# Last inverse-DFT stage of a long convolution for row pairs n2 and 98 - n2, with host-side layouts of the large operands

## The chip, the cores and the metric

The kernel runs on one core of one Trainium2 chip. The core has a matrix engine (PE, with its weight loads shown as PEld), three engines for elementwise work (DVE, ACT and POOL), and SP, which here only issues the transfers between the chip's main memory and the on-chip buffer. All transfers of this kernel stand in SP's one queue, in the order of the program; sixteen DMA engines carry them out. The metric is the device time of the core in microseconds; less is better.

## The reference

Two parts follow each other. The first is a gated long convolution over 12480 positions for 4 batches and 128 channels, done by FFT; the second is a feed-forward layer on the 49920 resulting rows.

```python
h_filt = (np.maximum(pos_emb @ w1, 0.0) @ w2) * np.exp(-0.01 * pos)[:, None]
u = x * v
Uf = np.fft.rfft(u, n=2 * S, axis=1)
Hf = np.fft.rfft(h_filt, n=2 * S, axis=0)
y = np.fft.irfft(Uf * Hf[None, :, :], n=2 * S, axis=1)[:, :S, :]
x2 = (x * y).reshape(B * S, D)
h = x2 @ w_in                                   # 128 -> 2048
g = h * np.clip(h + 3.0, 0.0, 6.0) / 6.0
return g @ w_out                                # 2048 -> 128
```

## The kernel before

**The transform.** The sequence is cut into two halves k of 98 and 97 rows (`R`) of 64 positions (`N1`), so that a position has a row index n2 and a column index n1. A transform has four matrix stages. `first_stage` (L223) multiplies 98 rows n2 of one channel by cosine and sine tables: the output is 64 rows for the cosine part and 64 for the sine part, each a float32 matmul on one half of the array's columns. `second_stage` (L242) goes over n1 with a table per frequency k2, 99 frequencies in 25 chunks of four. `products` multiplies with the filter's spectrum: two copies on ACT that swap real and imaginary parts (L474, L475), four products on DVE (L495 to L498), additions on POOL (L502). `third_stage` (L517) goes back over n1 and ACT copies the result into the buffer `z` (L525). `back` (L532) turns four columns of `z` with the identity so that k2 lies on the partitions, and `split_r` (L136 on ACT, L137 on DVE) splits the turned values into a high and a low part for matmuls of the reduced float32r type. `fourth_stage` (L551) takes eight columns: three products (high x high, high x low table, low x high) for the cosine and the sine part, six one-pass matmuls into one PSUM bank for 98 rows n2. ACT copies the bank to `y` (L557), and after 16 columns `store` (L567, L569) writes three blocks of 32 rows to `yd` and the one or two leftover rows to `ye`.

**The order.** Everything is emitted in a hand-written order and each engine keeps it. `filter` computes the filter's spectrum from `pos_emb` (64 turns L293, 16 hidden matmuls L305, then L327, which spreads over channels) and writes it to `hd`. Then come eight periods g, each for 2 batches x 32 channels. In a period, `chunk` goes through the 25 frequency chunks of group g; between the chunks the loop of `period` runs 32 steps n: a `back` of group g-1, sometimes a `fourth_stage` of group g-1, some decoding of feed-forward weights on DVE (`weight`, in periods 1 to 6), and after every fourth step a `visit`, which is four first stages of group g+1. x and v are loaded by `load_next` (L415) and multiplied by POOL in `gate_next` (L426). Tables `tab` (L446) are loaded 7 chunks ahead, the spectrum `h` (L459) 4 chunks ahead. `last_turn` does the turns and last stages of the last group, and `Moe.run` the feed-forward part: 98 tiles of 512 rows (two of them of leftover rows), each with 8 steps j of six matmuls up (L764 to L766) and six down (L799 to L803); x, y and the result of a tile are loaded and stored by `load` and `copy`.

**PSUM.** The eight banks are shared out by name: `BANKS = {"s2": 2, "sw": 1, "s3": 1, "ts": 3, "s4": 1}`. A name's banks are handed out in turn, and a matmul that starts in a bank waits until the last reader of the bank before is done. First stages and turns share "ts"; the last stage has "s4".

**Layouts.** x and v arrive as (batch, position, channel), so a load for 32 channels takes pieces of 32 values, 128 bytes; the same holds for the tiles of x and of the result in the feed-forward part.

Of the kernel before, what the change touches and what calls it, by code (L numbers as in the profile page):

```python
# [22 lines left out]

B, S, D = 4, 12480, 128
FO = 64
# [6 lines left out]
L = R[0] * N1  # L32

G = 32
GB = 2
GY = 16
NG = (D // G) * (B // GB)
# [5 lines left out]

NR = 3
REST = [(b, k, r) for b in range(B) for k in range(2) for r in range(32 * NR, R[k])]
# [15 lines left out]
def constants():  # L61
    n2, k2, n1, k1 = np.arange(R[0]), np.arange(K2), np.arange(N1), np.arange(N1)
    th = 2 * np.pi * np.outer(n2, k2) / N2
    c_tab = np.concatenate([np.cos(th), -np.sin(th)], axis=1)
    wt = np.where((k2 == 0) | (k2 == N2 // 2), 1.0, 2.0) / NF
    d_tab = np.stack([wt[:, None] * np.cos(th.T), -wt[:, None] * np.sin(th.T)], axis=1)
# [5 lines left out]
        [np.concatenate([fr, fi], axis=2), np.concatenate([-fi, fr], axis=2)], axis=0  # L72
    )
    ph = ph - (2 * np.pi / NF) * np.outer(k2, k1)[None]
    gr, gi = np.cos(ph), np.sin(ph)
    g_tab = np.concatenate(
# [16 lines left out]

@with_exitstack
def hyena_moe(ctx, tc, x, v, pos_emb, w1, w2, w_in, w_out, c_tab, d_tab, f_tab, g_tab, win_d, ident_d, out):
# [5 lines left out]
    yd = [[dram.tile([NR, 4, 32, 2, N1, GY], F32, name=f"yd{b}_{k}") for k in range(2)] for b in range(B)]  # L101
    ye = dram.tile([len(REST), N1, D], F32, name="ye")
# [8 lines left out]
    def rows(t, b, k, r0, r1):  # L111

        a = t[b, k * L + r0 * N1 : k * L + r1 * N1, :]
        return a.rearrange("(r n) d -> r n d", n=N1)

    left, right = ExitStack(), ExitStack()
    with tc.manual_schedule():
        conv = Conv(tc, nc, left, right, x, v, c_tab, d_tab, g_tab, ident, hd, yd, ye, rows, weights)
# [5 lines left out]
        moe = Moe(ctx, tc, nc, x, wd, yd, ye, out)  # L124
        conv.last_turn(moe)
        right.close()
        moe.run()
# [64 lines left out]
class Conv:  # L192
    def __init__(self, tc, nc, left, right, x, v, c_tab, d_tab, g_tab, ident, hd, yd, ye, rows, weights):
        self.tc, self.nc, self.left, self.right = tc, nc, left, right
        self.x, self.v, self.g_tab, self.ident, self.hd, self.yd, self.rows = x, v, g_tab, ident, hd, yd, rows
# [6 lines left out]
        self.dhi = self.keep.tile([K2, 2, R[0]], F32R, name="dhi")  # L202
        self.dlo = self.keep.tile([K2, 2, R[0]], F32R, name="dlo")
# [4 lines left out]
    BANKS = {"s2": 2, "sw": 1, "s3": 1, "ts": 3, "s4": 1}  # L208
# [38 lines left out]
    def filter(self, pos_emb, w1, w2, f_tab, win_d, ident_d):  # L247
# [11 lines left out]
        dtab = sp.tile([K2, 2, R[0]], F32, name="dtab")  # L259
# [8 lines left out]
        pt = flat[: R[0], : 2 * N1 * FO].rearrange("p (k n i) -> p k n i", k=2, n=N1)  # L268
        pos = [pos_emb[k * L : k * L + R[k] * N1, :].rearrange("(r n) i -> r n i", n=N1) for k in range(2)]

        def load_pos(n0, n1):
            for k in range(2):
                nc.sync.dma_start(pt[:96, k, n0:n1, :], pos[k][:96, n0:n1, :])

        nc.vector.memset(pt[96 : R[0], 1, :NB], 0.0)
        nc.gpsimd.memset(pt[96 : R[0], 1, NB:], 0.0)
        load_pos(0, NB)
        nc.sync.dma_start(self.ident, ident_d)
        for k in range(2):
            nc.sync.dma_start(pt[96 : R[k], k], pos[k][96:])  # L280
        for k in range(2):
            nc.sync.dma_start(w1bd[k * FO : (k + 1) * FO, k * FO : (k + 1) * FO], w1)
        for n in ((NB, 8), (8, 16), (16, 32), (32, N1)):
            load_pos(*n)
# [5 lines left out]
        def turned(n):  # L290
            tp = self.bank("ptT")
            for i in range(NB):
                nc.tensor.transpose(  # L293
                    tp[:, i * R[0] : (i + 1) * R[0]],
                    pt[:, i // 2, n + i % 2 * 2 : n + i % 2 * 2 + 2, :].rearrange("p n i -> p (n i)"),
# [17 lines left out]
        while pend:  # L313
            hidden(*pend.pop(0))
# [552 lines left out]
```

## Time and profile before

| | us |
|---|---|
| median of 3 runs | 3317.9 (3316.59 to 3318.12) |
| the profiled execution | 3315.44 |
| its span, first to last instruction | 3313.7 |
| first L764 (feed-forward part begins) | 1184.75 |
| first and last third-stage copies L525 | 180.0 and 1138.0 |

The page gives, per engine, the time in which it was busy and the number of instructions; forty slices of the span with tenths of busy time; and groups of instructions by source line with their count, total, mean in ns, and the idle time of the engine just before them. A time line row gives the start, the time until the last of the merged instructions ended, the engine, the line, what was written from what, the count, and in brackets the idle time before and what ended it. Matmuls overlap, so their distance from start to start is the price of one, not the duration in the row. A row of the window table gives a window, its length, the busy time and count of PE, PEld, DVE, ACT and POOL, the granted clock of PE as a share, the share of time in which the DMA engines moved data, and GB/s. A row of the waits names who waited for whom, and gives the sum in us, the count and the longest.

### The profile page before, as it was taken

Reading aid. Unit: us, or ns where it says so; the run is one execution under the profiler, and the core shown is the slowest. Engines: PE = TensorE matmul, PEld = TensorE weight load, DVE = VectorE, ACT = ScalarE, POOL = GpSimd, SP = SyncE. Lnnn points to the kernel's source line nnn. Section 1 sums busy time; section 2 is a strip of 40 time slices with the busy share of each in tenths; the row PEclk is TensorE's granted clock in tenths of the full one; section 3 lists DMA queues with packets and bytes.
Section 4 is the critical chain, followed back from the end, with each engine's and each line's share of the span. In section 5 each row is a group of like instructions: output and inputs, shape, how many; then the busy total and the mean of one; then the engine's idle time right before and its main releaser. Section 6 shows DMA issues by size and latency. Waiting matters only on the chain.

```text
span 3313.7 us, 54920 instructions
## 1 busy us (share of the span) xinstructions
PE 3226.8 (97%) x20346; PEld 2764.7 (83%) x20346; DVE 2380.8 (72%) x2837; ACT 2400.2 (72%) x3104; POOL 2108.6 (64%) x1243
## 2 busy tenths in 40 slices
PE   8988999999999999999999999999999999999999
PEld 7988888888888888888888888888888888888887
DVE  5545666666766667777777777777777777777776
ACT  2355666666667677778778787787878777777777
POOL 1166677676776546666666666666666666666666
PEclk9998999999999999999999999999999999999999
DMA  9789989989985522211211222112221112221121
GB/s 208 200 163 187 187 186 193 187 194 186 189 186 168 170 61 39 39 33 34 45 34 34 39 39 39 34 34 38 39 39 37 32 37 39 39 39 32 36 39 23
DMA packets 972127, 296.41 MB, mean 89 GB/s; under 512 B 841962, under 2 KB 938641, under 8 KB 970769
## 3 DMA queue, kind: packets, MB, share of 16 engines
q1 hardware_dynamic: 971860, 292.91, 42.1%
q8 instruction: 160, 2.62, 0.4%
q14 instruction: 107, 0.88, 0.1%
HBM read 224.49 MB, written 68.29 MB: 88 GB/s over the span
## 4 chain that ended last, share of the span: by engine, by line
PE 68%; POOL 0%; DVE 0%; issue 0%; ACT 0%
PE acc L803 11%; PE ph L764 11%; PE acc L800 11%; PE ph L765 11%; PE acc L799 11%; PE ph L766 11%; PE s L551 1%; PE ts L532 1%; PE s L517 1%; PE s L242 1%; PE s L532 0%; POOL pa L502 0%; DVE o L816 0%; ACT oT L806 0%; DVE wlo L137 0%
## 5 line engine op out<-in xcount | busy, mean ns | idle before, releaser
L788 POOL TENSOR_TENSOR glo<-g,ghi 128x1024 fp32r<-128x1024 f32 x588 | 1404.3, 2395 | 766.5 <-ACT ghi L786 766.3
L776 DVE SCALAR_TENSOR_TENSOR g<-r,ph 128x1024 f32<-128x1024 f32 (+1 forms) x784 | 949.5, 1211 | 411.1 <-ACT r L774 411.0
L774 ACT ACTIVATE r<-ph,three 128x1024 f32<-128x1024 f32 (+1 forms) x784 | 870.9, 1111 | 274.1 <-PE ph L766 274.0
L786 ACT CAST ghi<-g 128x1024 fp32r<-128x1024 f32 (+1 forms) x784 | 811.0, 1034 | 0.8 <-DVE g L776 0.7
L764 PE MATMUL ph<-xhi,win_hi 128*128 128x512 f32 (+1 forms) x1568 | 608.4, 388 | 0.0
L765 PE MATMUL ph<-xlo,win_hi 128*128 128x512 f32 (+1 forms) x1568 | 608.3, 388 | 0.0
L766 PE MATMUL ph<-xhi,win_lo 128*128 128x512 f32 (+1 forms) x1568 | 608.3, 388 | 0.0
L800 PE MATMUL acc<-ghi,wout_lo 128*128 128x512 f32 (+1 forms) x1568 | 608.0, 388 | 0.0
L799 PE MATMUL acc<-ghi,wout_hi 128*128 128x512 f32 (+1 forms) x1568 | 607.9, 388 | 0.0
L502 POOL TENSOR_TENSOR pa<-pa,pq 128x256 f32<-128x256 f32 (+1 forms) x400 | 312.5, 788 | 274.7 <-DVE pa L496 234.3
L803 PE MATMUL acc<-glo,wout_hi 128*128 128x512 f32 (+1 forms) x1568 | 481.2, 388 | 0.0
L764 PEld LDWEIGHTS ph<-xhi,win_hi 128*128 128x128 f32 x1568 | 294.3, 188 | 60.9 <-DVE g L776 0.2
L799 PEld LDWEIGHTS acc<-ghi,wout_hi 128*128 128x128 f32 x1568 | 294.4, 188 | 60.7
L765 PEld LDWEIGHTS ph<-xlo,win_hi 128*128 128x128 f32 x1568 | 294.5, 188 | 60.5
L766 PEld LDWEIGHTS ph<-xhi,win_lo 128*128 128x128 f32 x1568 | 294.4, 188 | 60.5
L800 PEld LDWEIGHTS acc<-ghi,wout_lo 128*128 128x128 f32 x1568 | 294.3, 188 | 60.4
L803 PEld LDWEIGHTS acc<-glo,wout_hi 128*128 128x128 f32 x1568 | 293.5, 188 | 60.9 <-POOL glo L788 0.7
L495 DVE TENSOR_TENSOR pq<-s,h 128x256 f32<-128x256 f32 (+1 forms) x200 | 84.2, 421 | 284.2 <-issue 106.3
L788 DVE TENSOR_TENSOR glo<-g,ghi 128x1024 fp32r<-128x1024 f32 x196 | 283.6, 1447 | 0.0
L223 PEld LDWEIGHTS ts<-ctab,u 98*64 98x64 f32 (+1 forms) x5120 | 229.4, 139 | 46.4 <-DVE wlo L137 24.9
L223 PE MATMUL ts<-ctab,u 98*64 98x99 f32 (+1 forms) x5120 | 246.8, 254 | 21.3 <-DVE wlo L137 20.8
L517 PE MATMUL s<-pa,tab 128*128 128x128 f32 x1694 | 240.9, 288 | 26.7 <-POOL pa L502 14.8
(72 smaller groups left out, 4060.0 us busy)
## 6 DMA issues: line engine op xcount, KB each, us to landing
tab<-in_g_tab SPq DMA_DIRECT2D x192, 256.0 KB
h<-hd SPq DMA_DIRECT2D x384, 128.0 KB
xt<-in_x SPq DMA_DIRECT2D x64, 384.0 KB
vt<-in_v SPq DMA_DIRECT2D x64, 384.0 KB
yd<-y SPq DMA_DIRECT2D x192, 128.0 KB
xt<-in_x SPq DMA_DIRECT2D x384, 64.0 KB
yt<-yd SPq DMA_DIRECT2D x96, 256.0 KB
out<-o SPq DMA_DIRECT2D x384, 64.0 KB
```

Source lines behind the costliest of these rows:

```text
L223: nc.tensor.matmul(tv[c * N1 : (c + 1) * N1, i, :K2], u[: R[k], 4 * j + i, :], self.ctab[: R[k], c * K2 : (c + 1) * K2], start=True, stop= ...
L502: nc.gpsimd.tensor_tensor(out=x, in0=x, in1=y, op=add)
L764: nc.tensor.matmul(ph[:, i, :ne], self.win_hi[:, sl], hi[:, :ne], start=True, stop=False)
L765: nc.tensor.matmul(ph[:, i, :ne], self.win_hi[:, sl], lo[:, :ne], start=False, stop=False)
L766: nc.tensor.matmul(ph[:, i, :ne], self.win_lo[:, sl], hi[:, :ne], start=False, stop=True)
L774: nc.scalar.activation(r[:, :, :ne], ph[:, :, :ne], AF.Relu, bias=self.three)
L776: nc.vector.scalar_tensor_tensor(out=g[:, :, :ne], in0=r[:, :, :ne], scalar=6.0, in1=ph[:, :, :ne], op0=ALU.min, op1=ALU.mult)
L786: nc.scalar.copy(ghi[:, :, :ne], g[:, :, :ne])
L788: e.tensor_tensor(out=glo[:, :, :ne], in0=g[:, :, :ne], in1=ghi[:, :, :ne].bitcast(F32), op=ALU.subtract)
L799: nc.tensor.matmul(a, self.wout_hi[:, f, :], ghi[:, i, :ne], start=(f == 0), stop=False)
L800: nc.tensor.matmul(a, self.wout_lo[:, f, :], ghi[:, i, :ne], start=False, stop=False)
L803: nc.tensor.matmul(a, self.wout_hi[:, f, :], glo[:, i, :ne], start=False, stop=(f == NFC - 1))
```

## The change

**The last stage.** For real results, the cosine part of the inverse DFT is the same for the rows n2 and 98 - n2 of the two halves' grid, and the sine part differs in sign. The change keeps tables for rows 0 to 49 only (`RH` = 50, padded to 64), computes the two parts into two banks and gets both rows as their sum and their difference. The parities of the frequency k2 are folded into the other tables. The matmuls are float32, without a split into high and low parts; each writes 64 output rows, and the two groups of 8 columns (h) go to the two halves of the array's columns.

```diff
-    BANKS = {"s2": 2, "sw": 1, "s3": 1, "ts": 3, "s4": 1}
+    BANKS = {"s2": 2, "sw": 1, "s3": 1, "ts": 4}
...
     def back(self, g, col):
...
-        if col % 8 == 0:
-            self.pair = [self.wp.tile([K2, 8, 128], F32R, tag=n, name=f"w{n}", bufs=3) for n in ("hi", "lo")]
-        hi, lo = (w[:, col % 8 : col % 8 + 4, :].rearrange("p c m -> p (c m)") for w in self.pair)
-        split_r(nc, hi, lo, t[:K2, :])
-        if col % 8:
-            self.pend.append((g, col - 4, *self.pair))
+        if col % GY == 0:
+            self.w = self.wp.tile([K2, GY, 128], F32, tag="w", name="w", bufs=3)
+        nc.scalar.copy(self.w[:, col % GY : col % GY + 4, :].rearrange("p c m -> p (c m)"), t[:K2, :])
+        if col % GY == GY - 4:
+            self.pend.append((g, col + 4 - GY, self.w))
...
+        g, col, w = self.pend.pop(0)
+        same, other = (self.bank("ts") for i in range(2))
+        for c, t in enumerate((same, other)):
+            for h in range(2):
+                nc.tensor.matmul(
+                    t[64 * h : 64 * h + 64, :],
+                    self.dtab[:, c, :],
+                    w[:, GH * h : GH * h + GH, c * N1 : (c + 1) * N1],
+                    start=True,
+                    stop=True,
+                )
+        y = self.wp.tile([128, 2, N1, GH], F32, tag="y", name="y")
+        same, other = (t.rearrange("p (c n) -> p n c", c=GH) for t in (same, other))
+        o = self.wp.tile([128, N1, GH], F32, tag="o", name="o", bufs=1)
+        nc.scalar.copy(o, other)
+        for i, op in enumerate((ALU.add, ALU.subtract)):
+            nc.vector.tensor_tensor(out=y[:, i], in0=same, in1=o, op=op)
...
+        for h in range(2):
+            e = ch // GH + h
+            for i, p, q, r, n in PARTS:
+                nc.sync.dma_start(self.yd[b][k][q, d // G, r : r + n, e], y[64 * h + p : 64 * h + p + n, i])
+            for i, p, r in ((0, 49, 49), (1, 1, 97)):
+                if r < R[k]:
+                    nc.sync.dma_start(
+                        self.ye[REST.index((b, k, r)), d // GH + e].unsqueeze(0), y[64 * h + p : 64 * h + p + 1, i]
+                    )
```

with `G` = 32, `GY` = 16, `GH` = 8, and the row blocks

```diff
+ROWS = [*range(32), *range(96, 64, -1), *range(32, 49), *range(64, 49, -1)]
+REST = [(b, k, r) for b in range(B) for k in range(2) for r in (49, 97) if r < R[k]]
+PARTS = [(0, 0, 0, 0, 32), (1, 2, 1, 0, 32), (0, 32, 2, 0, 17), (1, 34, 2, 17, 15)]
```

**Its place.** In a period the last stage now stands after every fourth step, right before the visit; one is left over for the next period's first chunk. In the last turn it comes with every fourth turn, which alternate between "ts" and "s2".

```diff
-                if len(self.pend) > 1:
-                    self.fourth_stage(self.pend.pop(0))
-                if g:
                     self.weight(n)
                 n += 1
-                if n % VISIT == 0 and g + 1 < NG:
-                    self.visit(g + 1, n // VISIT - 1)
+                if n % VISIT == 0:
+                    if n > VISIT:
+                        self.fourth_stage()
+                    if g + 1 < NG:
+                        self.visit(g + 1, n // VISIT - 1)
```

**Layouts.** The host hands over x and v by groups, so that a row of a load is 16 channels x 64 positions in one piece; x once more by tiles of the feed-forward part; `pos_emb` already turned; and it takes the result by tiles. The turns of `pos_emb` on PE and their copies on DVE go.

```diff
-                nc.sync.dma_start(t[r0:r1], self.rows(src, b, k, r0, r1)[:, part, d : d + G])
+                nc.sync.dma_start(t[r0:r1], src[g, piece, half, r0:r1])
...
-            self.nc.gpsimd.tensor_tensor(
-                out=u[: R[k], :, part].rearrange("p g n -> p n g"), in0=xt[: R[k]], in1=vt[: R[k]], op=ALU.mult
-            )
+            u = self.gated[-1][:, half * G // 2 : (half + 1) * G // 2, :]
+            self.nc.gpsimd.tensor_tensor(out=u, in0=xt, in1=vt, op=ALU.mult)
...
-        for n in range(0, N1, NB):
-            pend.append((n, turned(n)))
-            if len(pend) > 2:
-                hidden(*pend.pop(0))
-        while pend:
-            hidden(*pend.pop(0))
+        for n in range(0, N1, NB):
+            hidden(n)
...
-        self.copy(xt, self.x, t)
+        nc.sync.dma_start(xt, self.x[t])
...
+                for m in range(len(i)):
+                    a = self.ye[s + m, 4 * j : 4 * j + 4].rearrange("e (h r) c -> r h e c", r=32)
+                    for h in range(2):
+                        cols = slice(64 * m + 32 * h, 64 * m + 32 * h + 32)
+                        nc.sync.dma_start(
+                            y[32 * j : 32 * j + 32, cols].rearrange("r (e c) -> r e c", c=GH), a[:, h]
+                        )
...
-        self.copy(o, self.out, t)
+        nc.sync.dma_start(self.out[t, :, :ne], o[:, :ne])
```

The work that builds these layouts and puts the result back into its order is done in numpy outside the kernel and is not in the time: `by_groups`, `by_tiles`, `by_pairs` and `from_tiles` are reshapes, transposes and copies.

More of the change, by code (lines that the diff above doesn't have):

```diff
@@ L75, in constants @@
     gr, gi = np.cos(ph), np.sin(ph)
+    gr = np.where(oc, -gr, gr)
     g_tab = np.concatenate(
@@ L109, in hyena_moe @@
     ident = const.tile([P, P], F32, name="ident")
-    def rows(t, b, k, r0, r1):
-        a = t[b, k * L + r0 * N1 : k * L + r1 * N1, :]
-        return a.rearrange("(r n) d -> r n d", n=N1)
     left, right = ExitStack(), ExitStack()
     with tc.manual_schedule():
-        conv = Conv(tc, nc, left, right, x, v, c_tab, d_tab, g_tab, ident, hd, yd, ye, rows, weights)
+        conv = Conv(tc, nc, left, right, x, v, c_tab, d_tab, g_tab, ident, hd, yd, ye, weights)
         conv.filter(pos_emb, w1, w2, f_tab, win_d, ident_d)
@@ L192, with __init__ @@
 class Conv:
-    def __init__(self, tc, nc, left, right, x, v, c_tab, d_tab, g_tab, ident, hd, yd, ye, rows, weights):
+    def __init__(self, tc, nc, left, right, x, v, c_tab, d_tab, g_tab, ident, hd, yd, ye, weights):
         self.tc, self.nc, self.left, self.right = tc, nc, left, right
-        self.x, self.v, self.g_tab, self.ident, self.hd, self.yd, self.rows = x, v, g_tab, ident, hd, yd, rows
+        self.x, self.v, self.g_tab, self.ident, self.hd, self.yd = x, v, g_tab, ident, hd, yd
         self.c_tab, self.d_tab, self.weights, self.ye = c_tab, d_tab, weights, ye
@@ L360, in filter @@
                 self.gate_next()
-        split_r(nc, self.dhi, self.dlo, dtab)
         for piece in range(2 * GB):
@@ L409, in load_next @@
         piece, half = divmod(i, 2)
-        k, b, d = self.place(g, piece)
-        xt, vt = ((xv or self.xv).tile([R[0], N1 // 2, G], F32, tag=f"{c}t", name=f"{c}t") for c in "xv")
-        part = slice(half * N1 // 2, (half + 1) * N1 // 2)
+        xt, vt = ((xv or self.xv).tile([R[0], G // 2, N1], F32, tag=f"{c}t", name=f"{c}t") for c in "xv")
         for t, src in ((xt, self.x), (vt, self.v)):
-            for r0, r1 in ((0, 96), (96, R[k])):
-                nc.sync.dma_start(t[r0:r1], self.rows(src, b, k, r0, r1)[:, part, d : d + G])
-        self.loaded.append((k, part, xt, vt, xv is None))
+            for r0, r1 in ((0, 96), (96, R[0])):
+                nc.sync.dma_start(t[r0:r1], src[g, piece, half, r0:r1])
+        self.loaded.append((half, xt, vt, xv is None))
         self.n_loaded += 1
@@ L544, in fourth_stage @@
         piece, ch = divmod(col, G)
         k, b, d = self.place(g, piece)
-        d, ch = d + ch // GY * GY, ch % GY
-        t = self.bank(("s4", "s3")[col // 8 % 2] if g == NG - 1 else "s4")
-        n = 0
-        for wt, dt in ((hi, self.dhi), (hi, self.dlo), (lo, self.dhi)):
-            for c in range(2):
-                nc.tensor.matmul(
-                    t[: R[0], :], dt[:, c, :], wt[:, :, c * N1 : (c + 1) * N1], start=(n == 0), stop=(n == 5)
-                )
-                n += 1
@@ L855 @@
     arrays, args = {}, []
-    given = {n: np.ascontiguousarray(inputs[n]) for n in _INS} | constants()
+    x = np.asarray(inputs["x"])
+    given = {
+        "x": by_groups(x),
+        "v": by_groups(np.asarray(inputs["v"])),
+        "xt": by_tiles(x),
+        "pos_emb": by_pairs(np.asarray(inputs["pos_emb"])),
+    }
+    given |= {n: np.ascontiguousarray(inputs[n]) for n in ("w1", "w2", "moe_w_in", "moe_w_out")} | constants()
     for name, a in given.items():
```

180 lines of the change are left out of this document (78 added, 102 removed).

## The prediction

> **What bounds the kernel now.** I read the page first (busy shares and the forty slices), then the window table by stage, then the time line of PE inside one period, then the waits.
>
> ```profile
> PE 3226.8 (97%) x20346; PEld 2764.7 (83%) x20346; DVE 2380.8 (72%) x2837; ACT 2400.2 (72%) x3104; POOL 2108.6 (64%) x1243
> ...
> PEclk9998999999999999999999999999999999999999
> DMA  9789989989985522211211222112221112221121
> GB/s 208 200 163 187 187 186 193 187 194 186 189 186 168 170 61 39 39 33 34 45 34 34 39 39 39 34 34 38 39 39 37 32 37 39 39 39 32 36 39 23
> ```
>
> The page says PE everywhere, but two regimes lie under it: in the first thirteen slices (83 us each) the DMA engines are nearly full at only some 190 GB/s, afterwards they are almost idle. The window table cuts the span by stage: period 0, periods 1 to 6, period 7, the last turn, the feed-forward part (MoE).
>
> ```profile
> core 0: us, PE busy (x) PEld busy (x) DVE busy (x) ACT busy (x) POOL busy (x), PEclk, DMA share, GB/s
> ...
> 180.00:284.20 104.20, 89.90 (x1002) 85.04 (x1002) 48.40 (x100) 56.70 (x109) 70.58 (x72) 0.93 0.94 178
> 284.20:1049.20 765.00, 716.39 (x6803) 646.88 (x6804) 512.62 (x968) 508.26 (x948) 540.33 (x497) 0.96 0.88 187
> 1049.20:1138.00 88.80, 84.57 (x573) 77.24 (x572) 63.91 (x125) 64.04 (x117) 63.40 (x70) 0.99 0.59 180
> 1138.00:1184.70 46.70, 46.18 (x230) 39.56 (x231) 23.66 (x35) 29.13 (x50) 0.00 (x0) 0.95 0.45 120
> 1184.70:3313.70 2129.00, 2123.09 (x9409) 1758.74 (x9408) 1642.53 (x1369) 1687.16 (x1764) 1404.28 (x588) 1.00 0.19 37
> ```
>
> MoE is PE at full clock with no gap: 9408 matmuls in 2129 us, which the change neither adds to nor takes from. All that can move lies in the first 1185 us. There a period takes 765/6 = 127.5 us, with clock 0.96. How much of that is work? The starts on PE:
>
> ```profile
> 712.84 2.96 PE L223 MATMUL ts<-ctab,u 98*64 98x99 f32 x64
> 715.73 0.94 PE L532 MATMUL ts<-ident,z 128*99 128x128 f32 x4
> 716.51 1.06 PE L517 MATMUL s<-pa,tab 128*128 128x128 f32 x8
> ...
> 718.89 0.70 PE L551 MATMUL s<-whi,dhi 99*98 99x512 f32 x2
> 719.43 0.62 PE L551 MATMUL s<-whi,dlo 99*98 99x512 f32 x2
> 719.89 0.62 PE L551 MATMUL s<-wlo,dhi 99*98 99x512 f32 x2
> 720.35 1.05 PE L517 MATMUL s<-pa,tab 128*128 128x128 f32 x8
> 721.25 1.06 PE L242 MATMUL s<-z,tab 128*128 128x128 f32 x8
> ```
>
> From start to start: a chunk's four third-stage matmuls take 0.90 us (8 records, so a float32 matmul is two passes), a last stage (six one-pass matmuls, 8 columns) 720.35 - 718.89 = 1.46, four first stages (32 matmuls) 715.73 - 712.84 = 2.89, four turns 0.78. A period holds 25 chunks at 2 x 0.90, 32 turns at about 0.7, 16 last stages and 8 visits: 45 + 22 + 23 + 23 = 113 us. Some 14 us per period are waits and a lowered clock. The waits of PE, periods 1 to 6, then period 0:
>
> ```profile
> PE ts L223 <- DVE wlo L137: 20.8, 21, 1.9
> PE s L517 <- POOL pa L502: 10.4, 11, 1.5
> PE s L242 <- DMA tab<-in_g_tab: 9.9, 6, 3.1
> ...
> PE s L242 <- DMA tab<-in_g_tab: 13.2, 8, 3.1
> ```
>
> **The new last stage on PE.** It does 16 columns with four float32 matmuls of 99 rows by 64 output columns, 512 long: eight passes, each on one half of the array. The first stage is the same form, 98*64. Its 64 passes took 2.89 us, 45.2 ns a pass of 99 columns; whole-array passes (L517) take 0.90/8 = 112 ns for 128. Per column 0.456 against 0.879 ns: the two halves run at once. A pass of 512 columns is then worth 45.2 x 512/99 = 0.234 us, eight 1.87, and 0.10 for the change from whole to half array (estimate): 1.97 us against 2 x 1.46 = 2.92. Gain 0.95 each, 64 in all: 8 per period, 7.6 us. Bounds: 1.75 (whole-array speed halved, no overhead) and 3.84 (no overlap).
>
> At its beginning the first stage shows two passes started together:
>
> ```profile
> 712.84 0.31 PE L223 MATMUL ts<-ctab,u 98*64 98x99 f32 x2
> ```
>
> If the two passes of one matmul stand next to each other in the stream and none may start ahead of another, eight passes would take five slots of 0.467 and not four: 2.43 us. The Trainium skill, "TensorE: Matmul & The Clock Gate", Part 3: Packing small matmuls — row/col tiling, says just this of matmuls, "strict FIFO, no reordering"; by it the sum would be 0.46 x 64 = 30 us worse. The pair of first starts above speaks for four slots, so I take 1.97.
>
> **What the other engines lose and gain.** Means of one:
>
> ```profile
> L496 DVE TENSOR_TENSOR pa<-s,h 128x512 f32<-128x512 f32 x192 | 130.7, 680 | 0.0
> L557 ACT COPY y<-s 98x512 f32<-98x512 f32 x128 | 75.1, 586 | 82.4 <-PE s L551 77.0 <-DMA h<-hd 3.1 <-DMA xt<-in_x 0.8
> L137 DVE TENSOR_TENSOR wlo<-ts,whi 99x512 fp32r<-99x512 f32 x244 | 164.1, 683 | 63.6 <-ACT whi L136 62.9
> L426 POOL TENSOR_TENSOR u<-xt,vt 98x1024 f32<-98x1024 f32 x32 | 77.3, 2416 | 51.2 <-DMA vt<-in_v 50.5 <-POOL u L426 0.7
> ```
>
> Per period DVE loses 32 wlo (21.9 us) and gets 16 add/subtract of 128x512, nearest row 680 ns (10.9). ACT keeps 32 copies (w for whi) and does 8 copies o instead of 16 y: -4.7. POOL's u keeps its elements; only its output order changes, price as before. None of these busy times reaches PE's: POOL, the fullest, has 540/6 = 90 us a period.
>
> **The wait that goes and the wait that comes.** Today the first stages wait for a bank that wlo still reads. The long ones:
>
> ```profile
> 355.65 0.91 PE L223 MATMUL ts<-ctab,u 97*64 97x99 f32 x16 [0.52 <-DVE wlo L137]
> 358.44 2.91 PE L223 MATMUL ts<-ctab,u 97*64 97x99 f32 x32 [1.89 <-DVE wlo L137]
> ```
>
> wlo is gone, so 20.8/6 = 3.5 us a period go. But the new last stage takes two of the four "ts" banks and a visit of four first stages follows it at once. Ten banks are handed out per round, so the visit's third first stage gets the bank "same". That is free only after ACT's o (0.59) and both DVE operations (0.62 from start to start, then 0.68): 1.9 us after the last pass ends, while PE is there after two first stages, 2 x 0.72 = 1.4. Wait: about 0.6 us with idle engines (estimate), seven times a period 4.4, plus some 0.8 at the two visits where the weights' decoding has filled DVE: 6.0 us a period. Behind the waiting matmul stand the next chunk's matmuls on PE. Behind the two DVE operations stand the next products (L495 to L498), for which POOL waits. Bounds: 0 (if it hides) and 12 (DVE 1 us late each time).
>
> **The transfers.** x and v came in pieces of 128 bytes and come in rows of 4 KB; pos_emb, the MoE tiles and the result come in long rows too. Around 26 us, where f_tab's long rows run, the engines move
>
> ```profile
> 26.00:30.00 4.00, 4.00 (x22) 2.65 (x21) 1.70 (x3) 2.26 (x5) 0.00 (x0) 1.00 0.99 422
> ```
>
> 422 GB/s against 187 in the periods. So waits for tab go: 9.9/6 = 1.7 us a period, 13.2 in period 0. Clock: 0.96 of 127.5 is 5.1 us lost per period, 0.93 of 104.2 is 7.3 in period 0. I suppose that it sinks where PE idles long; those sources go, short ones come: I take 3.2 and 3.8 back (bounds 0 and all).
>
> What the change adds is issues on SP. Its queue now (xt and vt of one piece; yd three and ye one store; h; tab):
>
> ```profile
> 598.00 5.26 SPq L415 DMA_DIRECT2D xt<-in_x  x2
> 603.30 2.48 SPq L415 DMA_DIRECT2D vt<-in_v  x2
> 605.88 1.45 SPq L567 DMA_DIRECT2D yd<-y  x3
> 607.38 0.69 SPq L569 DMA_DIRECT2D ye<-y  x1
> 608.17 1.29 SPq L459 DMA_DIRECT2D h<-hd  x2
> 609.56 0.54 SPq L446 DMA_DIRECT2D tab<-in_g_tab  x1
> 610.20 1.23 SPq L459 DMA_DIRECT2D h<-hd  x2
> ```
>
> Start to start: h pair 1.36 and tab 0.64, 50 us a period; x and v 7.9 for four, later 32 x 0.50 = 16; weights 3. Stores: 4 last stages of 12 and 4 of 10 are 88 a period (32 before), at yd's 0.50: 44. Sum 113 of the 117.5 that I expect for the period. SP is covered, barely; its loads are ahead by 4 chunks (h) and 7 (tab), so its waits for DVE cost nothing by themselves.
>
> **Start, end and MoE.**
>
> ```profile
> 28.18 2.17 PE L305 MATMUL h<-z,w1bd 128*128 128x392 f32 x6
> 30.18 14.14 PE L327 MATMUL h<-w2bd,ht 128*98 128x128 f32 x128
> ```
>
> The position filter's 64 turns and their copies go. Left are 16 matmuls at 2.00/3 = 0.67 us = 10.7, after the first landing at some 5 us, and about 3 us (estimate) for slower first matmuls and the 3.2 MB to come: L327 starts near 18.7, 11.5 earlier (bounds 8 and 13). In MoE the loads and stores shrink to three per tile, off the path. The tile of eight leftover rows needs 64 loads from ye; now:
>
> ```profile
> 1515.55 1.90 SPq L718 DMA_DIRECT2D yt<-ye  x4
> ```
>
> At 0.48 that is 31 us, against some 31 us from SP's turn to the gate on DVE; 1 us for it (bounds 0 and 12). The last store is one issue, not four: -1.5.
>
> **Sum.** Start -11.5. Period 0: -13.2 - 3.8 = -17. Periods 1 to 6: -7.6 - 3.5 - 1.7 - 3.2 + 6.0 = -10.0 each, -60. Period 7 (15 last stages there, 8 after): 15.8 - 21.9 = -6.1. Last turn (17, then 9): 17.7 - 24.8 = -7.1. End -1.5, MoE +1. Together -102 on a span of 3313.7; the median of the runs, 3317.9, is 4.2 above it: 3216 us.
>
> **Rivals.**
> - Clean periods: the bank wait hides, the clock stays full, half of POOL's waits go. 127.5 - 7.6 - 3.5 - 1.7 - 5.1 - 0.9 = 108.7, or -113 for six: 3163. For it: DVE gets 11 us lighter. Against: o, add and subtract are a chain.
> - Periods stay: the new bank wait and POOL's lateness eat all: -60 falls away, 3276. For it: 10.4 us of POOL waits already now.
> - Five slots: the first-in-first-out order above, +30: 3246. It is the skill's rule just named; the pair of starts is against it.
> - SP becomes the bound. At ye's spacing (608.17 - 607.38 = 0.79) for every store its period is 69 + 70 = 139 us, +21 x 6 = 126: 3342, slower. It binds from (117.5 - 69)/88 = 0.55 us per store, and the kernel is slower than before from about 0.74. For it: 24 of the 88 move a single row, as ye does. Against: ye's row is cut into 64-byte pieces, the new one isn't.
> - The halves don't overlap at 512 columns: 3.84 us each, +120: 3336, slower; it decides from 1.97 + 102/64 = 3.56 us. Against: L223's rate.
>
> **Chances.** Forecast 0.45, clean 0.22, stay 0.12, five slots 0.07, SP 0.10 (half of it slower), no overlap 0.04. The first four and a short SP bind give faster 0.91; same (within 0.2%, 6.6 us, about what a measurement of this kernel can tell) 0.02; slower 0.07. Range 3155 to 3278: both clean and stay periods lie in it, the two slower cases are left out.
>
> **What would show it.** The time line after: a last stage of about 2 us between starts; L327 starting near 19 us; no wait for tab; L223 waiting on DVE's second operation at the third first stage of a visit, 0.6 us; periods of 117 us; MoE still 2129 us. I am wrong if periods stay near 127 (then the wait named there tells which engine), if the last stage takes 2.4 or 3.8, or if SP has no gap left.

## The result, and the profile after

The changed kernel takes 3259.49 us (median, 3254.63 to 3260.52); the kernel before, run beside it, 3317.24 us. The ratio is 0.9827, with a 95% interval of 0.981 to 0.9844. It became faster by 58 us, where 102 had been forecast; the forecast of 3216 us is 43 us too low, and its range of 3155 to 3278 holds the time.

The window table of the changed kernel, cut as the one of before was: period 0, periods 1 to 6, period 7, the last turn, the feed-forward part.

```profile
core 0: us, PE busy (x) PEld busy (x) DVE busy (x) ACT busy (x) POOL busy (x), PEclk, DMA share, GB/s
169.10:261.00 91.90, 84.04 (x1012) 79.92 (x1013) 48.35 (x100) 56.35 (x108) 69.55 (x72) 1.00 0.87 217
261.00:988.20 727.20, 663.99 (x6603) 581.50 (x6602) 480.00 (x872) 475.99 (x899) 515.93 (x497) 0.97 0.73 195
988.20:1074.20 86.00, 79.64 (x539) 66.68 (x538) 53.20 (x107) 58.27 (x109) 63.21 (x70) 0.99 0.54 155
1074.20:1120.90 46.70, 43.36 (x200) 27.96 (x200) 12.21 (x19) 23.92 (x42) 0.00 (x0) 0.95 0.51 170
1120.90:3257.30 2136.40, 2126.49 (x9409) 1760.61 (x9408) 1642.55 (x1371) 1687.37 (x1764) 1404.32 (x588) 1.00 0.12 37
```

Set beside the windows of before, stage by stage:

| us | forecast | measured | |
|---|---|---|---|
| up to period 0 | -11.5 | -10.9 | 180.0 to 169.1 |
| period 0 | -17 | -12.3 | 104.2 to 91.9 |
| periods 1 to 6 | -60 | -37.8 | 765.0 to 727.2, 121.2 each |
| period 7 | -6.1 | -2.8 | 88.8 to 86.0 |
| last turn | -7.1 | 0 | 46.7 to 46.7 |
| feed-forward part and end | -0.5 | +7.4 | 2129.0 to 2136.4 |
| sum | -102 | -56.4 | span 3313.7 to 3257.3 |

The time line of PE inside a period shows a last stage between a turn and a visit:

```profile
541.51 0.84 PE L557 MATMUL ts<-ident,z 128*99 128x128 f32 x4
542.28 1.94 PE L574 MATMUL ts<-w,dtab 99*64 99x512 f32 x8
544.05 2.92 PE L282 MATMUL ts<-ctab,u 98*64 98x99 f32 x64
546.89 0.94 PE L557 MATMUL ts<-ident,z 128*99 128x128 f32 x4
```

From start to start the new last stage takes 544.05 - 542.28 = 1.77 us, four slots, close to the lower bound of 1.75. PE has won more here than forecast. The waits of PE in periods 1 to 6 show where it went:

```profile
PE s L542 <- POOL pa L527: 22.1, 38, 1.6
PE s L301 <- DMA tab<-in_g_tab: 19.1, 11, 3.1
PE ts L557 <- DVE y L586: 15.3, 5, 3.5
PE s L301 <- DVE pa L521: 2.6, 1, 2.6
PE s L542 <- ACT sw L499: 2.3, 1, 2.3
PE s L542 <- ACT z L550: 1.0, 6, 0.2
```

The 20.8 us for wlo are gone, as forecast. But the waits for the tables, which were to vanish, doubled (9.9 before), those for POOL doubled too (10.4 before), and a new one stands in the third row: a turn that waits for y. There is no row in which a first stage (L282) waits for anything. All rows together are 62.6 us, against 48.6 before: the waits grew by 14.

### The profile page after: what moved, and what is told of

The parts are those of the page before. It is cut to its first block, busy times and chain, and to the rows that moved or that the text cites. A ratio compares the mean times of both kernels' runs of the same rounds, so it can differ in the third digit from the quotient of the medians.

```text
span 3257.3 us, 53858 instructions
## 1 busy us (share of the span) xinstructions
PE 3156.4 (97%) x20026; PEld 2667.5 (82%) x20026; DVE 2315.7 (71%) x2691; ACT 2356.5 (72%) x3039; POOL 2079.7 (64%) x1242
## 4 chain that ended last, share of the span: by engine, by line
PE 66%; DMA 1%; SPq 0%; POOL 0%; ACT 0%; issue 0%; DVE 0%; DVEq 0%; ACTq 0%
PE acc L807 11%; PE acc L803 11%; PE acc L804 11%; PE ph L769 11%; PE ph L770 11%; PE ph L768 11%; DMA yd<-y 1%; PE ts L574 0%; PE ts L557 0%; SPq L592 0%; PE s L557 0%; DMA yt<-yd 0%; PE s L542 0%; PE s L301 0%; DMA ye<-y 0%; DMA tab<-in_g_tab 0%
## 5 line engine op out<-in xcount | busy, mean ns | idle before, releaser
L527 POOL TENSOR_TENSOR pa<-pa,pq 128x256 f32<-128x256 f32 (+1 forms) x400 | 290.3, 732 | 247.4 <-DVE pa L521 220.8
L542 PEld LDWEIGHTS s<-pa,tab 128*128 128x128 f32 x1694 | 212.4, 197 | 64.4 <-POOL pa L527 50.0
L741 DVE TENSOR_TENSOR xy<-xt,yt 128x512 f32<-128x512 f32 x96 | 260.3, 2711 | 0.0
```

The costliest lines, as they stand in the source:

```text
L527: nc.gpsimd.tensor_tensor(out=x, in0=x, in1=y, op=add)
L542: nc.tensor.matmul(t[:, i * 128 : (i + 1) * 128], tab[:, i, :], a[:, i].rearrange("p s g -> p (s g)"), start=(n == 0), stop=(n == len(term ...
```

## Experiments

Each kernel was timed in three rounds beside the kernel before. The ratio is to that; the other columns are windows of its trace, cut as above, in us. The kernel before came out between 3317 and 3323 us in these rounds, so a few us between the medians of two rows say little by themselves; the ratios and the windows say more.

| kernel | median | ratio (95%) | to period 0 | period 0 | periods 1 to 6 | period 7 | last turn | feed-forward |
|---|---|---|---|---|---|---|---|---|
| before | 3317.24 | 1 | 180.0 | 104.2 | 765.0 | 88.8 | 46.7 | 2129.0 |
| changed | 3259.49 | 0.9827 (0.981 to 0.9844) | 169.1 | 91.9 | 727.2 | 86.0 | 46.7 | 2136.4 |
| e1 | 3284.57 | 0.989 (0.9874 to 0.9907) | 168.9 | 92.1 | 760.6 | 88.8 | 46.6 | 2127.0 |
| e2 | 3416.14 | 1.029 (1.0275 to 1.0305) | 169.2 | 102.3 | 873.9 | 85.9 | 46.6 | 2133.9 |
| e3 | 3232.24 | 0.9736 (0.9722 to 0.9751) | 168.7 | 92.0 | 712.6 | 85.2 | 42.5 | 2129.5 |
| e4 | 3257.52 | 0.9813 (0.9796 to 0.9829) | 169.2 | 92.0 | 732.2 | 86.0 | 46.9 | 2132.7 |
| e5 | 3259.21 | 0.9808 (0.9792 to 0.9824) | 169.6 | 92.0 | 731.8 | 86.0 | 48.2 | 2135.2 |
| e6 | 3262.4 | 0.9816 (0.9802 to 0.9831) | 169.9 | 92.0 | 732.5 | 85.3 | 42.6 | 2141.7 |
| e7 | 3184.57 | 0.9583 (0.9567 to 0.9599) | 169.1 | 92.0 | 667.1 | 83.1 | 41.6 | 2129.5 |
| c2 | 3209.41 | 0.9657 (0.9642 to 0.9671) | 168.2 | 92.0 | 690.1 | 86.0 | 42.8 | 2128.6 |
| e8 | 3208.5 | 0.9656 (0.9641 to 0.967) | 169.2 | 92.0 | 688.8 | 86.1 | 42.7 | 2128.6 |
| c3 | 3222.27 | 0.9694 (0.9678 to 0.9711) | 184.8 | 91.5 | 688.9 | 85.3 | 42.7 | 2129.5 |
| c4 | 3222.96 | 0.9701 (0.9686 to 0.9715) | 182.1 | 91.5 | 688.4 | 86.0 | 42.9 | 2129.6 |
| c5 | 3204.15 | 0.9645 (0.9629 to 0.9661) | 170.1 | 92.0 | 683.4 | 85.2 | 42.2 | 2128.6 |

### e1: the layouts alone

The kernel before, with the host-side layouts of the change and the old last stage; the core of the edit is

```diff
-                nc.sync.dma_start(t[r0:r1], self.rows(src, b, k, r0, r1)[:, part, d : d + G])
+                nc.sync.dma_start(t[r0:r1], src[g, piece, half, r0:r1])
...
-        self.copy(o, self.out, t)
+        nc.sync.dma_start(self.out[t, :, :ne], o[:, :ne])
```

> The layouts alone: x, v, pos_emb, the feed-forward tiles and the result as in the changed kernel, the last stage and its stores as before (six float32r matmuls for eight columns, four stores per sixteen columns). If the layouts carry the start, period 0 and the waits for tab, as the changed kernel's stages say (-11 at the start, -12 in period 0), and a part of the periods: periods of about 125 us, last turn 46.7 and feed-forward part 2129 us as before, 3277 us in all. If the new last stage carries the gain of the periods as well as most of the rest: periods of 127, some 3292 us.

The time lies between the two expectations. The start (-11.1), period 0 (-12.1) and the end (-2.0) come whole from the layouts. In periods 1 to 6 they bring 4.4 us and no more, though the waits for the tables vanish there; the waits of PE are now

```profile
PE ts L266 <- DVE wlo L180: 20.2, 20, 1.9
PE s L528 <- POOL pa L513: 18.1, 19, 2.3
PE s L528 <- ACT sw L485: 9.2, 4, 2.3
```

The 9.9 us that stood on the tables have moved to POOL (10.4 before) and to ACT's swap (6.5 before). A wait that is removed here comes back at the next engine in the chain.

### e2: the changed kernel with the old loads of x and v

```diff
-                nc.sync.dma_start(t[r0:r1], src[g, piece, half, r0:r1])
+                nc.sync.dma_start(t[r0:r1], self.rows(src, b, k, r0, r1)[:, part, d : d + G])
...
-            self.nc.gpsimd.tensor_tensor(out=u, in0=xt, in1=vt, op=ALU.mult)
+            u = self.gated[-1]
+            self.nc.gpsimd.tensor_tensor(
+                out=u[: R[k], :, part].rearrange("p g n -> p n g"), in0=xt[: R[k]], in1=vt[: R[k]], op=ALU.mult
+            )
```

> The changed kernel, but x and v loaded in pieces of 128 bytes and multiplied as before. If SP's issue is what long rows relieve: h 34, tab 16, x and v 48, stores 33, weights 3 make 134 us of SP a period, so periods of 134 us or more, about 3350 us, slower than before. If only the DMA engines' bandwidth counts: periods near 124, period 0 back at 104 us, about 3290 us.

873.9 / 6 = 145.7 us a period, and one wait of PE makes most of the difference:

```profile
PE s L306 <- DMA tab<-in_g_tab: 131.4, 40, 6.0
```

SP's rows in the time line, added over periods 1 to 6, are 755 us of 873.9 in 1205 issues (before: 666 of 765 in 873; changed: 516 of 727 in 1197). The DMA engines were no fuller than in the kernel before (a share of 0.79 at 164 GB/s, against 0.88 at 187), which speaks for SP being late and against the bandwidth, though SP's issues alone make only 126 of the 145.7 us. The new last stage brings so many stores that, with the old loads, the kernel takes 97 us more than the kernel before beside it (3319.55). All the layouts together bring 4 us in periods 1 to 6 under the old last stage (e1); the long rows of x and v alone bring 147 us (873.9 - 727.2) under the new one.

### e3: half the stores

The rows are put into two blocks of 48 instead of four blocks of 32, 32, 17 and 15, so that a last stage issues six stores instead of ten or twelve, of the same bytes. The feed-forward part loads a tile's y in four issues instead of one.

```diff
-            for i, p, q, r, n in PARTS:
-                nc.sync.dma_start(self.yd[b][k][q, d // G, r : r + n, e], y[64 * h + p : 64 * h + p + n, i])
-            for i, p, r in ((0, 49, 49), (1, 1, 97)):
-                if r < R[k]:
-                    nc.sync.dma_start(
-                        self.ye[REST.index((b, k, r)), d // GH + e].unsqueeze(0), y[64 * h + p : 64 * h + p + 1, i]
-                    )
+            for i in range(2):
+                p = 64 * h + i * (k + 1)
+                nc.sync.dma_start(self.yd[b][k][d // G, RM * i : RM * i + RM, e], y[p : p + RM, i])
+            m = REST.index((b, k, RM))
+            nc.sync.dma_start(self.ye[m : m + 2 - k, d // GH + e], y[64 * h + RM : 64 * h + RM + 2 - k, 0])
```

> The changed kernel with six stores per last stage in place of ten to twelve (48 rows of the sum and 48 of the difference in one store each, the leftover rows 48 and 49 in one), and four loads of y per feed-forward tile instead of one. If SP's many stores hold the y buffers and with them the last turn and the beginning of the feed-forward part: last turn 39 us instead of 46.8, feed-forward part 2129 to 2131 instead of 2136, periods 0 to 1 us shorter; 3244 us. If the chain o, add, subtract sets the last turn: no stage moves by more than 2 us, 3258 us.

It is 27 us faster than the changed kernel: periods 1 to 6 -14.6, the last turn -4.2, the beginning of the feed-forward part -6.9. In periods 1 to 6 no table and no spectrum is waited for any more:

```profile
PE s L542 <- POOL pa L527: 25.6, 40, 2.3
PE ts L557 <- DVE y L586: 17.6, 10, 2.8
PE s L542 <- ACT sw L499: 6.9, 3, 2.3
```

SP's issues are 444 us in 961 instructions here, against 516 in 1197. Neither fills SP. What else held SP stands in its own waits. In every trace of this case the issues on SP raise eight semaphores (counters that an engine can wait for) in strict turn, and all but a few (20 of 2057 in the changed kernel) wait for their own one first: such an issue goes out only when the transfer eight issues before it has landed. So the first of these two rows of the changed kernel, periods 1 to 6, is stores that wait for a load of v issued eight places earlier; the second is stores that wait for their own y:

```profile
SPq L592 <- DMA vt<-in_v: 24.5, 25, 1.8
...
SPq L592 <- DVE y L586: 1.8, 4, 1.1
```

All rows of that table that name a transfer add up to 114 us; all in which a store waits for DVE, to 13. In e3 the rows that name a transfer add up to 59 us, and SP waits 69 us for POOL to free a buffer of x and v (6 in the changed kernel), so there it is ahead. A store takes one of the eight places for nearly as long whatever its size: one row is issued in 0.24 us and has landed 2.7 us after its issue began (median), 32 rows 2.9 us after. So the number of stores costs twice, in issues and in places: 516 + 114 of 727 us in the changed kernel, 444 + 59 of 713 here. Which of the two made the 14.6 us no run separates.

### e4: eleven buffers for the tables

```diff
-NT = 7
+NT = 11
...
-            self.w = self.wp.tile([K2, GY, 128], F32, tag="w", name="w", bufs=3)
+            self.w = self.wp.tile([K2, GY, 128], F32, tag="w", name="w", bufs=2)
```

> The changed kernel with 11 buffers for tab instead of 7 (tables loaded 8 chunks ahead rather than 4), w with two buffers instead of three to make room. If PE's 19 us of waits for tab in periods 1 to 6 come from too short a lead in the quick chunks at a period's start: they fall below 5 us and some of the lowered clock goes, periods 118 us, 3240 us. If the DMA engines are simply full at those moments: the waits stay or turn into waits of DVE for h, 3255 us or more.

`NT` counts buffers. A table is held from the second stage to the third, so with seven buffers its load stands four chunks ahead of its second stage in the order, with eleven, eight.

No gain. The waits of PE for tables are gone, and DVE's products now wait for the spectrum instead (5.2 us in the changed kernel), whose loads stand in the same queue (the row of DVE, then two of PE):

```profile
DVE pq L520 <- DMA h<-hd: 36.3, 12, 4.8
```

```profile
PE s L542 <- POOL pa L527: 29.7, 38, 2.3
PE s L301 <- DVE pa L521: 11.8, 9, 2.5
```

By itself this would also fit DMA engines that are full. But e3 moves the same bytes in periods 1 to 6, faster, and loses both waits, so it is SP's queue that is late, not one of its loads.

### e5 and c2: the weights' decoding behind the last stage

The wait of the turns for y has its cause in DVE's time line:

```profile
597.87 0.67 DVE L523 TENSOR_TENSOR pa<-sw,h 128x512 f32<-128x512 f32 x1
598.47 1.30 DVE L238 TENSOR_SCALAR dec<-raw 128x256 int32<-128x256 int32 x1
599.69 0.81 DVE L240 TENSOR_SCALAR dec<-dec 128x256 int32<-128x256 int32 x1
600.53 1.43 DVE L242 SCALAR_TENSOR_TENSOR dec<-dec 128x256 f32<-128x256 int32 x1
601.89 1.27 DVE L586 TENSOR_TENSOR y<-ts,o 128x512 f32<-128x512 f32 x2
```

```profile
603.22 0.95 PE L557 MATMUL ts<-ident,z 128*99 128x128 f32 x4 [3.53 <-DVE y L586]
```

Three decoding steps, 3.4 us, stand ahead of the add and subtract, which read the bank "same" ("other" is free after ACT's o). The matmul that waits for them is not a first stage but the turn after the visit. Both kernels move the decoding: e5 in the changed kernel, c2 in that of e3.

```diff
                 if g:
                     self.back(g - 1, 4 * n)
-                    self.weight(n)
                 n += 1
                 if n % VISIT == 0:
...
                         self.visit(g + 1, n // VISIT - 1)
+                if g:
+                    self.weight(n - 1)
```

> The changed kernel with one move: the steps of the weights' decoding are emitted behind the last stage and the visit of the same turn, not ahead of them. Theory 1 (the decoding that stands on DVE ahead of the last stage's add and subtract holds the two banks): PE's wait at the turns for DVE's y (15.3 us in periods 1 to 6) vanishes and nothing takes its place; periods 1 to 6 take 712 us instead of 727, the kernel 3244 us. Theory 2 (DVE has no slack there, so the same 15 us turn up as PE waiting for POOL's or DVE's pa): periods 1 to 6 stay at 724 to 730 us and the kernel at 3257 to 3262.

> Fewer stores (as in e3) and the weights' decoding behind the last stage (as in e5) together. If both delays are separate, the 17.6 us for which the turns wait for y in periods 1 to 6 of e3 go too: periods 1 to 6 take about 697 us, the kernel 3217 us. If the periods are set by POOL and DVE whatever their order, it stays at 3230 to 3234.

In e5 the turns' wait for y is gone and nothing is won. The time is close to theory 2 (731.8 us in periods 1 to 6), its reason is not: PE's wait for POOL falls to 12.6 us, and the tables take the time (two rows of its waits):

```profile
PE s L301 <- DMA tab<-in_g_tab: 41.9, 20, 4.1
PE s L301 <- DVE y L586: 1.5, 3, 0.7
```

In c2, where SP is eased, the same move brings 22.5 us in periods 1 to 6, and POOL's row remains, 31.8 us. That is better than expected (690.1 for 697). While SP is late, taking away the wait on DVE wins nothing; fewer stores win 14.6 us alone and 41.7 us (731.8 - 690.1) once the decoding is moved.

### e6: four y buffers

```diff
-        y = self.wp.tile([128, 2, N1, GH], F32, tag="y", name="y")
+        y = self.wp.tile([128, 2, N1, GH], F32, tag="y", name="y", bufs=4)
```

(and two buffers of w, as in e4)

> The changed kernel with four y buffers instead of two (w has two instead of three, to make room). Theory 1 (in the last turn and at the beginning of the feed-forward part the two y buffers, held by ten to twelve stores each, are what is late): the last turn goes from 46.8 to about 42 us, DVE's waits for yd<-y there vanish, the kernel comes to 3252 us. Theory 2 (SP's issuing itself is late, some 5 us of issues for each last stage): the last turn may shorten, but the last store is issued as late as before and the feed-forward part gives the time back; the kernel stays within 3 us of 3259.

The last turn shrinks by 4.1 us and the feed-forward part grows by 5.3. In the changed kernel, DVE waited in the last turn for y buffers that were still being stored; now it waits once for the first tile of x (one row of DVE's waits of each, first the changed kernel's):

```profile
DVE y L586 <- DMA yd<-y: 18.9, 5, 6.7
```

```profile
DVE g L780 <- DMA xt<-in_xt: 12.3, 1, 12.3
```

SP's time line of e6 shows why: the load of that tile stands behind all the stores, and the last of them goes out at 1135.6, 13 us after the last turn ended at 1122.3.

```profile
1134.11 1.47 SPq L592 DMA_DIRECT2D yd<-y  x4
1135.62 0.24 SPq L595 DMA_DIRECT2D ye<-y  x1
1135.98 0.36 SPq L713 DMA_DIRECT2D xt<-in_xt  x1
```

So in the last turn it is SP's issuing that is late; a buffer only moves the place where PE feels it. e3, with fewer issues, wins both back.

### e7, c3, c4 and c5: what is left, POOL

e7 halves POOL's sums in the kernel of e3; the other half of them is left out:

```diff
-            nc.gpsimd.tensor_tensor(out=x, in0=x, in1=y, op=add)
+            w = G // 2 if g else G
+            nc.gpsimd.tensor_tensor(out=x[..., :w], in0=x[..., :w], in1=y[..., :w], op=add)
```

> The kernel of e3 (fewer stores), in which POOL's additions of the products cover only half of the columns from period 1 on (the other half of those sums is left out of the computation). Theory 1 (POOL is what is late in the periods once SP is eased): the waits of PE for POOL's pa (25.6 us in periods 1 to 6) vanish, periods 1 to 6 go from 712.6 to about 690 us, the kernel from 3232 to 3210. Theory 2 (DVE's products are as late as POOL's sums, which only stand behind them): the waits turn to DVE's pa, periods 1 to 6 stay above 705 us and the kernel above 3224.

Theory 1 holds, and more strongly than expected: periods 1 to 6 fall by 45.5 us, beyond the 25.6 us of POOL's own row, because the waits for y (17.6 to 6.4) and the swap's (6.9 to none) shrink with it and the clock is granted in full, while the wait for ACT's z grows (1.6 to 13.2). But it isn't a test of POOL alone: DVE's busy time fell as well, from 482 to 438 us for the same 872 instructions, all of it in the weights' decoding (L242 from 1443 to 904 ns). How much of the gain is DVE's is open. c3 takes work from POOL in another way, to the kernel of c2 (`half` holds for the second half of a piece; two of the products moved, at 38 and 47 us, stand ahead of period 0):

```diff
-            self.nc.gpsimd.tensor_tensor(out=u, in0=xt, in1=vt, op=ALU.mult)
+            eng = self.nc.vector if again and half else self.nc.gpsimd
+            eng.tensor_tensor(out=u, in0=xt, in1=vt, op=ALU.mult)
```

> The kernel of c2, with every second product u = x*v (second half of a piece, from period 0 on) computed on DVE instead of POOL. If POOL is what is late in periods 1 to 6 (31.8 us of PE's waits, and e7 with half of POOL's sums got to 667 us): POOL is rid of about 23 x 2.41 = 55 us, DVE gets an estimated 23 x 1.4 = 32 us; periods 1 to 6 from 690 to about 670 us, the kernel 3189 us. If DVE's order counts as much (its products then come later, and POOL waits for them): 688 to 695 us, the kernel 3207 to 3214.

> The kernel of c3 with tables asked for nine chunks ahead (now seven) and three y buffers (two of w). If nothing is late on SP any more, as the waits of c2 say (none for tab, none for h): within 3 us of c3. If the buffers still count in the last turn: 2 to 5 us below c3.

c3's periods stay as they were (688.9 for 690.1), and 17 us are lost before period 0: for 10.7 of them PE waits for DVE, whose queue stands behind a product that waits for its load of v. c4, with more buffers on top, wins nothing. POOL was rid of 23 products in periods 1 to 6, some 55 us, but its busy time fell by 31 only (516 to 484), since its smaller sums took 814 ns in the mean and not 739: a pair that starts together with a product on DVE takes 2.43 us where others take 1.42. PE's wait for POOL fell from 31.8 to 21.8 us, and its wait for ACT's swap rose from 2.3 to 11.5. So work handed from POOL to DVE comes back as a wait elsewhere; what less work on POOL alone would bring, c3 doesn't tell. The time lines of POOL and PE in c2, at the beginning of a period, show one place where POOL is late:

```profile
490.85 1.27 POOL L527 TENSOR_TENSOR pa<-pa,pa 128x512 f32<-128x512 f32 x1
492.07 2.36 POOL L453 TENSOR_TENSOR u<-xt,vt 98x1024 f32<-98x1024 f32 x1
494.39 1.41 POOL L527 TENSOR_TENSOR pa<-pa,pq 128x256 f32<-128x256 f32 x2
495.88 1.27 POOL L527 TENSOR_TENSOR pa<-pa,pa 128x512 f32<-128x512 f32 x1
```

```profile
497.20 1.24 PE L542 MATMUL s<-pa,tab 128*128 128x128 f32 x8 [2.30 <-POOL pa L527]
```

In the first chunks of a period few turns stand between the chunks, and POOL needs more per chunk (about 2.7 us for three sums) than PE (2 x 0.9). The product u stands in just these chunks; it is a first half, which c3 had left on POOL. c5 moves it by one chunk:

```diff
-GATES = (1, 4, 8, 11, 14, 17, 20, 22)
+GATES = (2, 5, 8, 11, 14, 17, 20, 22)
```

> The kernel of c2, with the first two products u = x*v of each period from 1 on emitted one chunk later (chunks 2 and 5, not 1 and 4). Theory 1 (in the first chunks of a period, where PE has no turns to fill it, POOL's three sums of 2.9 us a chunk are what is late, and the product of 2.36 us ahead of them makes one wait of 2.30 us on PE per period): behind the product's new place PE has a visit to do, so that wait goes, periods 1 to 6 from 690 to 676 to 679 us, the kernel 3195 to 3199 us. Theory 2 (the chain of products, sums and PE is late by itself, the product only stands in it; c3 took 55 us from POOL without a gain): less than 4 us in all, the kernel 3205 to 3210 us.

Periods 1 to 6 get 6.7 us shorter, half of what theory 1 said and more than theory 2 did. The 2.30 us wait is gone, the longest is 1.4, but by the distances of ACT's copies L550 some 1.3 us a period come back four chunks later, behind the second product. The row that stays is

```profile
PE s L542 <- POOL pa L527: 29.5, 45, 1.4
```

many short waits. That POOL's chain of three sums makes their length is argued and not shown: in c2 DVE's products wait for POOL (98 us) and POOL's sums for DVE (148 us) in turn, and no run gave the products more buffers.

### e8: the halves apart

```diff
-        for c, t in enumerate((same, other)):
-            for h in range(2):
+        for h in range(2):
+            for c, t in enumerate((same, other)):
                 nc.tensor.matmul(
```

> The kernel of c2, with the last stage's four matmuls in another order: both of the array's lower output half first, then both of its upper half (now they alternate). Theory 1 (a matmul may start ahead of an earlier one that waits for the other half of the array): a last stage stays at 1.77 us from start to start, the kernel at 3209. Theory 2 (matmuls start in the order of the stream, and the four slots come from the alternation): the eight passes stand four by four and take seven slots of 0.43 to 0.47 us, about 3.1 us; 64 last stages cost 64 x 1.3 = 83 us more on PE, of which some hides in PE's waits (34 us in periods 1 to 6): 3255 to 3290 us.

Nothing changes. The time line of PE, first over the 0.35 us from the first start and then over the whole last stage:

```profile
512.84 0.66 PE L574 MATMUL ts<-w,dtab 99*64 99x512 f32 x2
```

```profile
512.84 1.94 PE L574 MATMUL ts<-w,dtab 99*64 99x512 f32 x8
514.61 2.92 PE L282 MATMUL ts<-ctab,u 98*64 98x99 f32 x64
```

Two passes start together though the first two matmuls of the stream are on one half, and the stage takes 514.61 - 512.84 = 1.77 us. The trace doesn't name the halves; that two passes together take no longer than one tells that they are on different ones. The halves work through their own matmuls side by side, whichever order they come in. The Trainium skill, "TensorE: Matmul & The Clock Gate", Part 3: Packing small matmuls — row/col tiling, has matmuls start in strict order; for float32 passes on two halves these runs do not agree: by the rule e8 would have needed seven slots, about 3.1 us.

**The best version** is c5: e3's stores, the decoding moved, the product one chunk later. 3204.15 us, ratio 0.9645 (0.9629 to 0.9661) to the kernel before, 117 us less than that took beside it (3321.24). The interval overlaps that of c2, so c5's last 5 us rest on the window of periods 1 to 6.

## Why the prediction was right, and where not

**Price of the last stage: right in its mechanism, a little too dear.** 1.97 us was forecast, 1.77 measured: the 0.10 for the change of array shape isn't there, and a pass is 0.43 and not 0.47 us for a pair. That is 8 x (2.92 - 1.77) = 9.2 us a period instead of 7.6. (The lower bound of 1.75 does not come out of its own figures: half of 0.879 ns times 8 x 512 is 1.80, and the time measured lies below that.) The rivals of five slots and of halves that don't overlap fall with the time line above and with e8.

**Start: right.** The spreading began at 19.34 us on the page's clock where 18.7 had been forecast; e1 has it at 18.7, so it is the layouts. No run shows the 3 us for slower first matmuls and the landing by itself; the sixteen matmuls took 14.2 us from 5.10 on, where 13.7 had been put down with it.

**wlo's waits: right**, they are gone. **The new bank wait: wrong place, half the size.** Forecast: the third first stage of every visit, 0.6 us, 6.0 us a period with idle engines. By banks handed out in turn the third first stage would get "same", and the trace says otherwise: in the visit ahead of the turn at 603.22 all four first stages and their copies are done by 600.2, while y is written until 603.16. Why, is not shown. No first stage waits, and in a quiet visit y is ready 0.7 us before the turn needs it: 544.88 + 1.29 = 546.17 in DVE's row, the turn at 546.89 in PE's time line above.

```profile
544.88 1.29 DVE L586 TENSOR_TENSOR y<-ts,o 128x512 f32<-128x512 f32 x2 [0.82 <-ACT o L584]
```

The wait comes only where the decoding is ahead on DVE, 15.3 / 6 = 2.6 us a period. The forecast had 0.8 for this.

**Tables and clock: the tables wrong.** They were to bring 1.7 us a period and cost 3.2 instead of 1.7. The lowered clock was to fall from 5.1 us a period by 3.2; 0.97 of 121.2 is 3.6, so it gave about 1.5 (the shares are rounded to 0.01, 1.2 us a period). With PE's waits it goes only roughly: 24 us of them in periods 1 to 6 of e7 and 33 in c5 go with 1.00, 164 in e2 with 0.89, but the kernel before has 0.96 at 48.6 and the changed one 0.97 at 62.6. What sets it is not shown. In period 0, where no stores run, both came true: no wait for tables, clock 1.00. There 17 us were forecast and 12.3 came. The row of 13.2 us for tables came from a window that reached to 290 us: 10.1 us of it lie in period 0, and the other 3.1 had been counted in the 9.9 of periods 1 to 6 as well. The clock gave back all of its 7.3 us instead of 3.8, and waits for ACT and POOL grew (8.7 us in these two rows, 4.4 before):

```profile
PE s L542 <- ACT z L550: 5.5, 9, 1.5
PE s L542 <- POOL pa L527: 3.2, 4, 1.1
```

**The step that failed** is this sentence: SP "is covered, barely; its loads are ahead by 4 chunks (h) and 7 (tab), so its waits for DVE cost nothing by themselves". The sum in it was too high (113 us a period; 516 / 6 = 86 were measured, a store being 0.37 us by 1.47 for four and not 0.50), and the conclusion was still wrong. Two things were wrong in it. The lead: 7, here and in the description of the kernel before, is the number of table buffers, and the order asks for a table four chunks ahead (e4). As it ran, when a table's load was issued, 1 to 4 chunks (2.4 in the mean) still stood between the last chunk whose swap on ACT (L499) had begun and the table's own; for h it was 0 to 3 (1.7). In e3 the means are 3.0 and 2.5. And SP's cost: only issues were counted, not the 114 us in which SP waited for the transfer eight issues earlier; stores that waited for DVE, which the sentence has in mind, were 13 us. So SP was not full and yet late. e3 prices the stores: 14.6 us in periods 1 to 6. The other 7.6 us of that stage's shortfall of 22 are not taken apart by a run; c2 and c5 show that moving DVE's decoding and POOL's product is worth 22.5 and 6.7 us once SP is eased.

**Luck in the sum.** Per period the last stage gave 9.2 us instead of 7.6, the tables cost 1.5 more than before instead of 1.7 less, the bank wait came to 2.6 instead of 6.0, the clock gave 1.5 instead of 3.2, and POOL's waits cost 2.0 more where nothing was put down. Errors of both signs cancel in part, and some 2 us a period stand in none of these rows. The direction and most of the mechanisms were right, but the time is nearer to the rival of unchanged periods (3276) than to the forecast (3216); that it lies in the range is in part luck.

**Last turn and feed-forward part: the same step.** Both were priced on PE alone (-7.1) and on the leftover tile (+1). But nine last stages of ten or twelve stores meet there, about 4 us of SP for each against 4.8 us on PE, and behind them stand the first tiles' loads. e3 gives back 4.2 and 6.9 us. The leftover tile's 64 loads did stay covered.

**Period 7** brought 2.8 of 6.1. No edit but e7's moved it below 85.2, so POOL's chain rather than SP may be what holds it; that is only argued.

**SP as a rival:** forecast with 0.10 as the bound that could make the kernel slower. e2 shows it at work (1.029), without the long rows. So the new last stage needs the long rows; the layouts do not need it, and alone they bring 35 us (e1, 3284.57 against 3319.55).

## What to carry to other kernels

Price a queue in program order by its waits and by the number of its transfers as well, not only by the sum of its issues: here SP issued for 71% of periods 1 to 6, an issue had to wait for the landing of the one eight before it, and the kernel lost 27 us to the number of its stores. Count a lead in chunks from the order of issue, not from the number of buffers. Where several engines form one chain, removing a wait that isn't the latest one brought nothing (e4, e5, e6), and the same edit pays once the later one is gone (c2): so ease the shared queue first and then try again what failed. The Trainium skill, "Trainium Kernel Development and Optimization", Key Constraints, says that issuing from several engines saves only the sequencer's issue time; issue time was part of what was late here, but no run put the stores on another engine's queue.

## What the runs showed of the hardware that was not expected

- Two float32 matmuls of 64 output columns on different halves of the array run at once whatever their order in the stream: eight passes of 512 columns in 1.77 us in both orders.
- Eight transfers of SP's queue are under way at most in these kernels, since issues use eight semaphores in turn, and a store of one row (2 KB, 2.7 us to landing) holds its place nearly as long as one of 32 rows (2.9 us).
- What an issue costs on SP goes by the number of its pieces far more than by their bytes. The two loads of one half of v took 2.48 us of SP in 128-byte pieces (the row stands in the prediction) and take 0.64 us in long rows, by this row of the changed kernel's SP time line; a store of 15 to 32 rows takes 0.37 us (1.47 for four).

```profile
515.10 0.64 SPq L442 DMA_DIRECT2D vt<-in_v  x2
```
